# Top 32 from pairs of scores in twelve steps, a shorter first load, and more score slots in an attention and two-expert-layer kernel

## The chip, the cores and the metric

The kernel runs on one core of one Trainium2 chip. The metric is the device time of one execution in microseconds; the kernel before took a median of 808.22 us in 3 runs (807.57 to 808.52).

## The reference

Three stages run one after the other. Cut to what matters:

```python
# q, k, v: batch 2, heads 8, seq 576, head_dim 64; top_k = 32
scores = scale * q @ k.T
kth = 32nd largest of each row of scores
scores = where(scores >= kth, scores, -1e9)
attn = softmax(scores)                       # over the kept ones
x = (attn @ v), heads side by side           # 1152 tokens x 512
x = sum over 4 experts e of p[:, e] * (relu(x @ w1[e]) @ w2[e])   # F = 1024
out = ((x @ w_a) * (x @ w_b)) @ w_out        # d_ff = 1536
```

Every row of 576 scores needs its largest score and its 32nd largest one; the rest follows from these two.

## The kernel before

The 1152 tokens are cut into nine tiles of 128, and the tiles into groups of 1, 2, 3 and 3 (`GROUPS`, L28). Attention runs in 36 steps: for each group, for each of the 4 pairs of heads, for each tile of the group. So steps 0 to 3 belong to the first group, 4 to 11 to the second, 12 to 23 to the third and 24 to 35 to the fourth. A group's expert layer can be finished only when all four pairs of heads of the group are through.

One step treats one tile and two heads (x = 0, 1). TensorE makes 128x576 scores for each head (`scores`, L760, asked for `AHEAD` = 2.4 steps early); ScalarE copies them from PSUM into a score slot (L781; four slots, L513). VectorE then finds the 32 largest in `masked` (`top`, L796): four times MAX8, which gives the eight largest of a row, and between them three times MATCH_REPLACE8, which overwrites those eight by a very low number in a copy in the buffer `e` (L815). So a head takes seven passes over 576 elements. `e` has three buffers (L516). GpSimd makes two small products from the largest and the 32nd largest (L829, L833); ScalarE passes over the 576 scores three times (L839 masks, L844 takes exponentials and their sum, L855 divides by the sum); GpSimd writes one column of `e` (L874) to mark it ready, TensorE transposes it in `weigh` (L885 to L898) and multiplies it with v. The result of a pair of heads goes into `xf` (first group) or as high and low part into `xs` (L935, L937).

The operands of a step are loaded `OPERANDS` = 3 steps early: k is read in two DMAs (one for each head; the very first in four, L655), turned by TensorE, and kept in a scratch in DRAM for later groups; the last 64 rows of k of both batches lie in `krem`, filled by four DMAs with the first k (L661 to L667), for which the first transposes wait. q comes in two DMAs for a tile. All DMAs are issued by SyncE's queue (`load`, L568).

The first group's expert layer (`plain`, L1169) uses plain fp32 weights; the others (`experts`, L1007) use weights split into a high part, cast by ScalarE (L958), and a low part, subtracted by GpSimd or, where `late` is set, by VectorE (L959, L961 to L963). `late` (L1018) is set for the whole fourth group and for the last two experts of the third.

The order of the work on every engine is fixed before the program is built: each operation is entered with an engine, an expected duration, a key, what it waits for and the buffers that it uses; a planner (`Plan.order`, L216) starts on each engine the ready operation of the smallest key for which its buffers are free, and `Plan.best` (L147) keeps the best of 42 such orders. Buffers of one kind are handed out in one fixed sequence. So any change of costs, keys or slots can change the order of everything that comes after.

The seven passes, as the program enters them:

```python
for r in range(rounds):                                   # L798
    ... nc.vector.max(m8v()[:, x, cs], at())              # L809
    if r < rounds - 1:
        ... nc.vector.match_replace(out=src[1](), in_to_replace=m8v()[:, x, cs],
                                    in_values=at(), imm_value=LOW)   # L815
```

Of the kernel before, what the change touches and what calls it, by code (L numbers as in the profile page):

```python
# [16 lines left out]
DRAM = bass.MemoryType.DRAM  # L17

TOPK = 32
LOW = -3.0e38  # L20
STEEP = 2.0**80
MIX = "mix"
# [4 lines left out]
SIZES = [1, 2, 3, 3]  # L27
GROUPS = [TILES[sum(SIZES[:i]):sum(SIZES[:i + 1])] for i in range(len(SIZES))]  # L28

AHEAD = 2.4  # L30
OPERANDS = 3.0

# [376 lines left out]
TURN_F = 109  # L409
AV, SWITCH = 1092, 350  # L410
SCORE, TILED = 1944, 190
LATE = 2

FILL = 9
SLACK, EASE = 1200, 600

URGENT = 3

SOONER = (99,)

# [8 lines left out]
def body(tc, q, k, v, probs, w1, w2, wa, wb, wo, out):  # L429
# [66 lines left out]
    wscr = dr.tile([F2 // 256, 128, 2048], F32, name="wscr")  # L496

    big = Region("big", 10752, F32)
    kts = big.slots("kt", 4, WK)
    kraws = big.slots("kraw", 2, M4 * 2 * D)  # L500
    krems = big.slots("krem", 2, H * D)
    qraws = big.slots("qraw", 2, 4 * 2 * D)
    qas = big.slots("qa", 2, 4 * 128)
    mid = Region("mid", 4 * 2048 + 5 * 768, F32)
    wides = mid.slots("wide", WIDE, 2048)
    mid.again(F32R)
# [9 lines left out]
    turns = [Typed(sb, f"e{i}", 2 * S) for i in range(3)]  # L516
    es = Slots("e", turns, "e", [(i * 2 * S, (i + 1) * 2 * S) for i in range(3)])
    es.rank = 0
    m8s = low.slots("m8", 2, 2 * TOPK)
    endss = low.slots("ends", 2, 4)  # L520
    sumss = low.slots("sums", 2, 2)
    hfs = low.slots("hf", 2, 512)
# [45 lines left out]
    def load(dst, src, key, after=(), tiles=(), nbytes=1 << 18, since=0.0):  # L568


        op = plan.add("SP", 0, lambda: nc.sync.dma_start(out=dst(), in_=src()), key, after, tiles, nbytes=nbytes)  # L571
        op.since = since
        return op

    def scalar(n, emit, key, after, tiles, sbuf=False, ptr=False, extra=0):
        return plan.add("ACT", act(n, sbuf, ptr) + extra, emit, key, after, tiles, lag=110)
# [26 lines left out]
    def main_rows(x, b, h):  # L603

        return x[b, h:h + 2, 0:MAIN].rearrange("h (p m) d -> p h m d", m=M4)
# [37 lines left out]

    vrem_done, qrem_done, kept = {}, [], {}
    krem = [krems.tile() for _ in range(B)]
    krem_done = []

    def keys(b, h2, key):

        h = 2 * h2  # L650
        rt, kt = kraws.tile(key), kts.tile(key)
        rv = lambda: rt.ap.rearrange("p (m h d) -> p m h d", h=2, m=M4)
        first_ = not krem_done
        lds = []
        for m0, m1 in ((0, 2), (2, M4)) if first_ else ((0, M4),):  # L655
            for i in range(2):
                lds.append(load(
                    lambda i=i, m0=m0, m1=m1: rv()[:, m0:m1, i], lambda i=i, m0=m0, m1=m1: main_rows(k, b, h)[:, i, m0:m1],
                    key - 2, (), [rt], 32768 * (m1 - m0),
                ))  # L660
        if first_:  # L661
            for c in range(B):
                for x in range(B):
                    rs = slice((x + c) % B * REM, ((x + c) % B + 1) * REM)
                    krem_done.append(load(
                        lambda c=c, rs=rs: krem[c].ap[rs].rearrange("p (h d) -> p h d", d=D), lambda x=x: last_rows(k, x), key - 1.98, (), [krem[c]], 131072,
                    ))  # L667
        at = atts.tile(key + 0.02)

        def turn():  # L670
            a = at.ap.rearrange("p c n -> p (c n)")
            kr = [krem[c].ap[:, h * D:(h + 2) * D] for c in (1 - b, b)]
            tr(a[:, 0:128], kr[0], ident)
            for m in range(M4):
                tr(a[:, (1 + m) * 128:(2 + m) * 128], rt.ap[:, m * 128:(m + 1) * 128], ident)
            tr(a[:, 640:768], kr[1], ident)

        o = tensor(6 * TURN_F, turn, key + 0.02, lds + krem_done + [ready], [at, rt] + krem)
        av = lambda c0, c1: at.ap.rearrange("p c n -> p (c n)")[:, REM + c0:REM + c1]
        if first_:  # L680
            got = [
                scalar(HALF + REM, lambda: nc.scalar.activation(kt.ap[:, 0:HALF + REM], av(0, HALF + REM), AF.Copy), -902, [o], [at, kt]),
                vector(dve(HALF), lambda: nc.vector.tensor_copy(kt.ap[:, HALF + REM:WK], av(HALF + REM, WK)), -902, [o], [at, kt]),
            ]
        else:
            got = [scalar(WK, lambda: nc.scalar.activation(kt.ap, av(0, WK), AF.Copy), -902, [o], [at, kt])]  # L686
        if any(c for c, g in enumerate(GROUPS) if (b, h2) not in kept and c >= 0):
            kept[b, h2] = load(lambda: kscr[b, h2], lambda: kt.ap, key + 1, got, [kt], 320 << 10, since=13e3)
        return kt, got
# [7 lines left out]
    def queries(pair, n, key):  # L697

        h, T = pair.h, pair.T
        norm = [t for t in pair.tiles if t != MIX]  # L700
        rq, qa = qraws.tile(key), qas.tile(n)
        rqv = lambda: rq.ap[:, 0:len(norm) * 128].rearrange("p (m h d) -> p m h d", m=len(norm), h=2)
        lds = []
        for b in sorted({t[0] for t in norm}):
            at = [i for i, t in enumerate(norm) if t[0] == b]
            r0, w = norm[at[0]][1], len(at)
            for i in range(2):
                lds.append(load(
                    lambda a0=at[0], w=w, i=i: rqv()[:, a0:a0 + w, i], lambda b=b, r0=r0, w=w, i=i: main_rows(q, b, h)[:, i, r0:r0 + w],
                    key - 1.95, (), [rq], 32768 * w,  # L710
                ))
        if MIX in pair.tiles:
            if not qrem_done:
                for b in range(B):
                    qrem_done.append(load(lambda b=b: qrem[b * REM:(b + 1) * REM], lambda b=b: last_rows(q, b), key - 2, (), (), 131072, since=60e3))
            lds += qrem_done
        at = ms.tile() if n == 0 else atts.tile(key + 0.04)
        a = lambda: (at.ap if n == 0 else at.ap[:, 0])[:, 0:T * 128]

        def turn():  # L720
            for i, t in enumerate(pair.tiles):
                tr(a()[:, i * 128:(i + 1) * 128], qrem[:, h:h + 2].rearrange("p h d -> p (h d)") if t == MIX else rq.ap[:, i * 128:(i + 1) * 128], ident)

        o = tensor(T * TURN_F, turn, key + (0.015 if n == 0 else 0.04), lds + [ready], [at, rq])
        if n == 0:
            pair.qd = [vector(dve(128), lambda: nc.vector.tensor_copy(qa.ap[:, 0:128], a()), -903, [o], [at, qa])]
        else:
            pair.qd = [scalar(T * 128, lambda: nc.scalar.activation(qa.ap[:, 0:T * 128], a(), AF.Copy), -901, [o], [at, qa])]
        pair.q = qa

    def start_pair(c, h2, n):
# [25 lines left out]
                ]  # L757
        return pair

    def scores(pair, i, n):  # L760

        t = pair.tiles[i]
        ats, ss_ = [atts.tile(n - AHEAD + 0.001 * j) for j in range(2)], [ss.tile(n + 0.001 * j) for j in range(2)]
        parts = [(slice(0, 128), t[0])] if t != MIX else [(slice(b * REM, (b + 1) * REM), b) for b in range(B)]

        def emit():
# [20 lines left out]
    def masked(sd, n):  # L787
# [5 lines left out]
        ev = lambda x: ep.ap[:, x * S:(x + 1) * S]  # L793
        last = []

        def top(x, src, c0, rounds, width, key, done):  # L796

            for r in range(rounds):  # L798
                cs = slice(c0 + r * 8, c0 + r * 8 + 8)
                at = src[min(r, 1)]  # L800
                if n + r == 0:
# [10 lines left out]
                if r < rounds - 1:  # L812
                    done = vector(
                        132 + 1.04 * width,
                        lambda at=at, cs=cs: nc.vector.match_replace(  # L815
                            out=src[1](), in_to_replace=m8v()[:, x, cs], in_values=at(), imm_value=LOW
                        ),
                        key + 0.02 * r + 0.01, done, [m8, sd[x][0], ep],
                    )
            return done[0]  # L820

        for x in range(2):
            s = sd[x][0]
            key = n + 0.001 * x
            last.append(top(x, [lambda s=s: s.ap, lambda x=x: ev(x)], 0, TOPK // 8, S, key, sd[x][1]))
        ks = -3000 + n if n in SOONER else n + 0.1 if n > URGENT else n - 0.7
        out_, ex = [], []
        en = gpsimd(
            150, lambda: nc.gpsimd.tensor_tensor(endv(), m8v()[:, :, ::TOPK - 1], facs.unsqueeze(2).to_broadcast([128, 2, 2]), op=ALU.mult),  # L829
            -500, last + [ready], [m8, ends]  # L830
        )
        off = gpsimd(
# [174 lines left out]
    def experts(c):  # L1007
# [7 lines left out]
        yd, sums_ = {}, {}  # L1015
        for e in range(E):

            late = 2 if c == len(GROUPS) - 1 else c == len(GROUPS) - 2 and e >= LATE  # L1018
            for f0 in range(0, F, 512):
                hts, units = [], []  # L1020
                for u in range(f0, f0 + 512, 256):
# [448 lines left out]
```

## Time and profile before

| | |
|---|---|
| median of 3 runs | 808.22 us (807.57 to 808.52) |
| the profiled execution | 808.02 us, of which the profile's span is 806.2 us |
| TensorE busy | 771.0 us (96%), mean granted clock 0.998 |
| VectorE busy | 731.9 us (91%) |
| ScalarE busy | 508.0 us (63%) |
| GpSimd busy | 238.0 us (30%) |
| chain that ended last | TensorE 87%, VectorE 7%, DMA 2% |

Busy time is that of the engine's own instructions; instructions of the sequencers (waits, DMA issues) are not in it. The chain is followed back from the last instruction, at each step to what released it. The span is divided in the page into 40 slices of some 20 us; TensorE's busy tenths in them begin 5, 6, 8 and are 9 in all later ones but the eighth and the last, which are 8.

### The profile page before, as it was taken

Reading aid. Unit: us, or ns where it says so; the run is one execution under the profiler, and the core shown is the slowest. Engines: PE = TensorE matmul, PEld = TensorE weight load, DVE = VectorE, ACT = ScalarE, POOL = GpSimd, SP = SyncE. Lnnn points to the kernel's source line nnn. Section 1 sums busy time; section 2 is a strip of 40 time slices with the busy share of each in tenths; the row PEclk is TensorE's granted clock in tenths of the full one; section 3 lists DMA queues with packets and bytes.
Section 4 is the critical chain, followed back from the end, with each engine's and each line's share of the span. In section 5 each row is a group of like instructions: output and inputs, shape, how many; then the busy total and the mean of one; then the engine's idle time right before and its main releaser. Section 6 shows DMA issues by size and latency. Waiting matters only on the chain.

```text
span 806.2 us, 14094 instructions
## 1 busy us (share of the span) xinstructions
PE 771.0 (96%) x5145; PEld 673.1 (83%) x5145; DVE 731.9 (91%) x1425; ACT 508.0 (63%) x871; POOL 238.0 (30%) x289
## 2 busy tenths in 40 slices
PE   5689999899999899999999999999999999999998
PEld 3477776688888778888899998899988989899996
DVE  4999999999999999999998599898899899999755
ACT  2688778899898889776675657566545533233110
POOL 0000014475666526430000001321224334343121
PEclk9999999999999999999999999999999999999999
DMA  5875887445654343433324455889521413313013
GB/s 146 264 260 162 291 254 237 151 141 182 199 164 159 107 143 105 142 127 102 109 78 131 157 172 170 271 296 323 180 106 42 137 32 106 124 34 105 0 54 117
DMA packets 100037, 122.57 MB, mean 152 GB/s; under 512 B 26624, under 2 KB 73728, under 8 KB 98432
## 3 DMA queue, kind: packets, MB, share of 16 engines
q1 hardware_dynamic: 99968, 121.67, 46.9%
q8 instruction: 40, 0.66, 0.4%
q14 instruction: 29, 0.24, 0.1%
HBM read 110.38 MB, written 11.27 MB: 151 GB/s over the span
## 4 chain that ended last, share of the span: by engine, by line
PE 87%; DVE 7%; DMA 2%; ACT 1%; SPq 1%; issue 0%; POOL 0%; DVEq 0%; ACTq 0%
PE ps L589 83%; PE ps L592 4%; DVE low L809 3%; DVE e L815 2%; DMA mid<-in_moe_w_dram 2%; SPq L571 1%; ACT lowa L901 0%; DMA big<-in_k_dram 0%; DVE mid_again L1031 0%; DVE xs L1163 0%; DVE low L1056 0%; ACT big L686 0%; ACT e L855 0%; ACT lowa L781 0%; DVE e L1272 0%
## 5 line engine op out<-in xcount | busy, mean ns | idle before, releaser
L589 PE MATMUL ps<-mid_again 128*128 128x512 f32 x1092 | 262.9, 393 | 0.0
L589 PEld LDWEIGHTS ps<-mid_again 128*128 128x128 f32 x1092 | 201.2, 188 | 43.8 <-issue 4.7
L589 PE MATMUL ps<-xs,mid_again 128*128 128x384 f32 (+1 forms) x1152 | 192.3, 320 | 4.7 <-DVE xs L1163 2.1
L589 PEld LDWEIGHTS ps<-xs,mid_again 128*128 128x128 f32 x1152 | 181.5, 189 | 12.4 <-issue 4.5
L809 DVE MAX8 low<-e 128x8 f32<-128x576 f32 x216 | 154.5, 748 | 0.0
L959 POOL TENSOR_TENSOR mid_again<-raw,mid_again 128x1024 fp32r<-128x1024 f32 x48 | 114.8, 2402 | 25.5 <-ACT mid_again L958 23.2
L958 ACT ACTIVATE mid_again<-raw 128x1024 fp32r<-128x1024 f32 x96 | 101.1, 1057 | 19.7 <-PE ps L589 12.6
L815 DVE MATCH_REPLACE8 e<-low,e 128x576 f32<-128x576 f32 x144 | 106.1, 743 | 0.0
L1275 POOL TENSOR_TENSOR low<-e,e 128x512 int32<-128x512 int32 x36 | 50.0, 1389 | 161.1 <-DVE e L1272 113.3
L589 PE MATMUL ps<-xs,big_again 128*128 128x320 f32 (+1 forms) x576 | 86.4, 297 | 0.2 <-DVE low L1364 0.2
L589 PEld LDWEIGHTS ps<-xs,big_again 128*128 128x128 f32 x576 | 80.3, 190 | 1.1 <-DVE low L1364 0.4
L589 PE MATMUL ps<-lowa_again,big_again 128*128 128x320 f32 (+1 forms) x432 | 66.4, 296 | 1.4 <-ACT rest L1373 1.1
L959 DVE TENSOR_TENSOR mid_again<-raw,mid_again 128x1024 fp32r<-128x1024 f32 x48 | 62.2, 1301 | 5.0 <-ACT mid_again L958 4.8
L1027 ACT ACTIVATE mid_again<-ps 128x384 fp32r<-128x384 f32 (+1 forms) x96 | 43.3, 455 | 33.6 <-PE ps L589 32.9
L589 PEld LDWEIGHTS ps<-lowa_again,big_again 128*128 128x128 f32 x432 | 60.8, 190 | 2.5 <-ACT rest L1373 1.3
L839 ACT ACTIVATE e<-lowa,low 128x576 f32<-128x576 f32 x72 | 53.1, 776 | 13.7 <-POOL low L829 13.3
L855 ACT ACTIVATE e<-e,low 128x576 f32<-128x576 f32 x72 | 52.7, 772 | 11.1 <-DVE low L852 11.0
L844 ACT ACTIVATE e<-e,low 128x576 f32<-128x576 f32 x72 | 55.6, 775 | 0.8 <-POOL low L833 0.7
L1031 DVE SCALAR_TENSOR_TENSOR mid_again<-ps,mid_again 128x384 fp32r<-128x384 f32 (+1 forms) x96 | 48.3, 506 | 7.4 <-ACT mid_again L1027 6.7
L1364 DVE TENSOR_TENSOR low<-ps,low 128x256 f32<-128x256 f32 (+1 forms) x105 | 43.7, 447 | 11.4 <-PE ps L589 10.8
L815 DVE MATCH_REPLACE8 e<-low,lowa 128x576 f32<-128x576 f32 x72 | 53.1, 743 | 0.0
L781 ACT ACTIVATE lowa<-ps 128x576 f32<-128x576 f32 x72 | 42.9, 644 | 13.0 <-PE ps L589 9.0
(110 smaller groups left out, 1013.2 us busy)
## 6 DMA issues: line engine op xcount, KB each, us to landing
raw<-in_moe_w_dram SPq DMA_DIRECT2D x116, 512.0 KB, 4.0
big<-kscr SPq DMA_DIRECT2D x20, 320.0 KB, 4.0
low<-in_v_dram SPq DMA_DIRECT2D x24, 256.0 KB, 3.7
e<-in_moe_w_b_dram SPq DMA_DIRECT2D x12, 512.0 KB, 4.2
e<-in_moe_w_a_dram SPq DMA_DIRECT2D x12, 512.0 KB, 3.9
e<-in_moe_w_out_dram SPq DMA_DIRECT2D x12, 512.0 KB, 4.3
wscr<-big_again SPq DMA_DIRECT2D x6, 1024.0 KB, 5.6
mid_again<-wscr SPq DMA_DIRECT2D x6, 1024.0 KB, 4.9
```

The source lines that it names most:

```text
L589: nc.tensor.matmul(out, l, r, **kw)
L809: 62 + 1.04 * width, lambda at=at, cs=cs: nc.vector.max(m8v()[:, x, cs], at()), key + 0.02 * r, [done],
L815: lambda at=at, cs=cs: nc.vector.match_replace(out=src[1](), in_to_replace=m8v()[:, x, cs], in_values=at(), imm_value=LOW),
L839: S, lambda x=x, s=s: nc.scalar.activation(ev(x), s.ap, AF.Prelu, bias=endv()[:, x, 1:2], scale=scale, alpha=STEEP),
L844: lambda x=x: nc.scalar.activation(ev(x), ev(x), AF.Exp, bias=endv()[:, x, 0:1], accum_out=sums.ap[:, x:x + 1]),
L855: S, lambda x=x: nc.scalar.activation(ev(x), ev(x), AF.Copy, scale=sums.ap[:, x:x + 1]),
L958: hi = scalar(1024, lambda: nc.scalar.activation(u.ap[:, 0:1024], r.ap, AF.Copy), 500 + s, [ld], [u, r], sbuf=True)
L959: sub = lambda eng: eng.tensor_tensor(u.ap[:, 1024:2048], r.ap, u.ap[:, 0:1024], op=ALU.subtract)
L1027: n, lambda h=h, p=p: nc.scalar.activation(h.ap[:, 0:n], p.ap[:, 0:n], AF.Relu), -1000, [o], [h, p]
L1031: lambda h=h, p=p: nc.vector.scalar_tensor_tensor(h.ap[:, n:2 * n], p.ap[:, 0:n], 0.0, h.ap[:, 0:n], op0=ALU.max, op1=ALU.subtract),
L1275: return gpsimd(pool_(512), lambda: nc.gpsimd.tensor_tensor(t().bitcast(I32), fold(c.ap.bitcast(I32)), fold(lowv().bitcast(I32)), op=ALU.a ...
L1364: return vector(dve(m), lambda: nc.vector.tensor_tensor(tv(out), p.ap[:, 0:m], tv(i), op=ALU.add), K, [o] + after, [p, tp])
```

## The change

- **First loads.** The first k is one DMA of both heads. The first `krem` part is only what the first pair of heads needs: of the 64 rows of the step's own batch one DMA for each copy, one issued by SyncE and one by ScalarE, the other 64 rows being set to zero by GpSimd; the remaining six DMAs for `krem` follow. The first q is one DMA, issued by ScalarE. Later k and one-tile q are one DMA instead of two.
- **Pairs of scores.** In steps 0 to 11 (without head 0 of step 0) the row is folded: VectorE takes the larger of score i and score i + 288 (`larger`), GpSimd adds the bit patterns of the two as integers (`added`) and subtracts the larger one (`smaller`), each over 288 elements. The top 32 of the larger ones take four MAX8 and three MATCH_REPLACE8 over 288, the top 16 of the smaller ones two and one. At most 16 of the 32 largest scores can be smaller ones of their pair, so the 32nd largest is the minimum over sixteen maxima of one sorted list against the other reversed: two small VectorE operations for a step. The three folding operations are asked for 1.99 steps early and use the step's buffer `e`. The first MATCH_REPLACE8 of the larger ones waits for `smaller` (`guard`).
- **Slots and keys.** Ten score slots instead of four, five k buffers instead of four; scores asked for 4.4 steps early, operands 5.
- **Low parts.** `late` is now set for the last two experts of the fourth group alone.

The diff, cut to its core:

```diff
+WM = 3 * TOPK // 2 + 2
-AHEAD = 2.4
-OPERANDS = 3.0
+AHEAD = 4.4
+OPERANDS = 5.0
-LATE = 2
+FOLD = range(12)
-    kts = big.slots("kt", 4, WK)
+    kts = big.slots("kt", 5, WK)
+    ss2 = big.slots("s2", 6, S)
-    m8s = low.slots("m8", 2, 2 * TOPK)
+    m8s = low.slots("m8", 2, 2 * WM)
+    def load_by_act(dst, src, key, tiles=()):
+        return plan.add("ACT", 100, lambda: nc.scalar.dma_start(out=dst(), in_=src()), key, (), tiles, lag=LAND)
...
-        for m0, m1 in ((0, 2), (2, M4)) if first_ else ((0, M4),):
-            for i in range(2):
-                lds.append(load(
-                    lambda i=i, m0=m0, m1=m1: rv()[:, m0:m1, i], lambda i=i, m0=m0, m1=m1: main_rows(k, b, h)[:, i, m0:m1],
-                    key - 2, (), [rt], 32768 * (m1 - m0),
-                ))
+        lds = [load(rv, lambda: pair_rows(k, b, h), key - 2, (), [rt])]
...
+                gpsimd(200, lambda c=c, blank_=blank_: nc.gpsimd.memset(krem[c].ap[blank_, 0:2 * D], 0.0), -1e5, [], [krem[c]])
+            krem_done[0] = [plan.ops[-1], plan.ops[-2], last(1, 0, 0, 2, key - 1.98), last(0, 0, 0, 2, -1e5, True)]
+            rest_ = [last(c, x, 2, H, key - 1.9) for x in range(B) for c in range(B)]
+            krem_done[1] = [last(c, 1, 0, 2, key - 1.9) for c in range(B)] + rest_
...
+            if n == 0:
+                lds.append(load_by_act(lambda: rqv()[:, 0], lambda b=b, r0=r0: pair_rows(q, b, h)[:, r0], -1e6, [rq]))
+            elif w == 1:
+                lds.append(load(lambda a0=at[0]: rqv()[:, a0], lambda b=b, r0=r0: pair_rows(q, b, h)[:, r0], key - 1.95, (), [rq], 65536))
...
+        folds = [x for x in range(2) if n in FOLD and (n, x) != (0, 0)]
         for x in range(2):
...
+            kf = n - 1.99 + 0.001 * x
+            added = gpsimd(pool_(HALF), lambda halves=halves, low_=low_: whole(nc.gpsimd, ALU.add, low_(), *halves()), kf, [sd[x][1]], [s, ep])
+            larger = vector(
+                dve(HALF) + 30, lambda halves=halves, high=high: nc.vector.tensor_tensor(high(), *halves(), op=ALU.max), kf, [sd[x][1]], [s, ep], port=True
+            )
+            smaller = gpsimd(
+                pool_(HALF), lambda high=high, low_=low_: whole(nc.gpsimd, ALU.subtract, low_(), low_(), high()), kf, [added, larger], [ep]
+            )
+            t = top(x, [high], [8 * r for r in range(TOPK // 8)], key, larger, smaller)
+            last.append(top(x, [low_], [TOPK, TOPK + 8], key + 0.09, smaller))
+            last[-1].waits.append(t)
+        if folds:
+            xs_ = slice(folds[0], folds[-1] + 1)
+            a = vector(
+                100, lambda: nc.vector.tensor_tensor(
+                    m8v()[:, xs_, TOPK // 2:TOPK], m8v()[:, xs_, TOPK // 2:TOPK], m8v()[:, xs_, 3 * TOPK // 2 - 1:TOPK - 1:-1], op=ALU.max
+                ), n + 0.15, last[folds[0]:], [m8]
+            )
+            last.append(vector(
+                100, lambda: nc.vector.tensor_reduce(
+                    out=m8v()[:, xs_, WM - 2:WM - 1], in_=m8v()[:, xs_, TOPK // 2:TOPK], axis=mybir.AxisListType.X, op=ALU.min
+                ), n + 0.16, [a], [m8]
+            ))
...
-            late = 2 if c == len(GROUPS) - 1 else c == len(GROUPS) - 2 and e >= LATE
+            late = 2 if c == len(GROUPS) - 1 and e >= 2 else 0
```

## Rows read from the trace of the kernel before

**Rows 1.** Windows: stretch, length, busy PE, PEld, DVE, ACT, POOL; clock; DMA share.
```profile
0.00:13.00 13.00, 6.13 (x24) 4.62 (x24) 1.29 (x4) 1.75 (x2) 1.94 (x11) 1.00 0.51 114
13.00:60.00 47.00, 33.49 (x232) 25.90 (x230) 46.48 (x100) 32.17 (x62) 2.65 (x15) 1.00 0.81 254
60.00:133.00 73.00, 72.14 (x527) 52.43 (x528) 71.63 (x159) 56.93 (x107) 11.64 (x32) 1.00 0.77 234
133.00:166.00 33.00, 28.63 (x201) 22.80 (x199) 32.74 (x72) 29.58 (x53) 14.74 (x19) 0.95 0.56 178
...
255.00:295.00 40.00, 36.02 (x273) 30.40 (x274) 39.52 (x86) 33.95 (x60) 16.54 (x20) 1.00 0.45 145
295.00:460.00 165.00, 165.00 (x1175) 144.89 (x1174) 151.84 (x289) 120.98 (x204) 36.82 (x56) 1.00 0.36 114
```

**Rows 2.** Chain that ended last: start us, length us, what.
```profile
4.88 3.44 DMA big<-in_k_dram
...
163.00 1.46 DVE e L815 x2
...
276.77 1.46 DVE e L815 x2
```

**Rows 3.** Timeline of DVE, 150 to 153 and 290 to 291: start, length.
```profile
150.89 0.41 DVE L937 TENSOR_TENSOR xs<-ps,xs 128x256 fp32r<-128x256 f32 x1
...
290.43 0.54 DVE L937 TENSOR_TENSOR xs<-ps,xs 128x384 fp32r<-128x384 f32 x1
```

**Rows 4.** Timeline of all engines, first 14 us.
```profile
0.71 4.80 SPq L571 DMA_DIRECT2D big<-in_k_dram  x8
...
5.56 1.09 SPq L571 DMA_DIRECT2D big<-in_q_dram  x2
...
8.45 1.73 PE L592 MATMUL ps<-identr,big 128*128 128x128 f32 x7 [4.16 <-DMA big<-in_k_dram]
...
10.88 2.29 PE L589 MATMUL ps<-big 64*128 64x288 f32 x8 [0.70 <-DVE big L726]
...
13.17 1.43 DVE L804 MAX8 low<-ps 128x8 f32<-128x576 f32 x2 [2.44 <-PE ps L589]
```

**Rows 5.** Timeline of DVE, 85 to 89 us: issue times of neighbours.
```profile
85.83 0.74 DVE L809 MAX8 low<-e 128x8 f32<-128x576 f32 x1
86.49 0.07 DVE L815 MATCH_VALUE_LOAD e<-low,e 128x8 f32 x1
...
87.21 0.08 DVE L815 MATCH_VALUE_LOAD e<-low,e 128x8 f32 x1
...
87.93 0.41 DVE L937 TENSOR_TENSOR xs<-ps,xs 128x256 fp32r<-128x256 f32 x1
88.26 0.15 DVE L852 RECIPROCAL low<-low 128x2 f32<-128x2 f32 x1
88.34 1.40 DVE L809 MAX8 low<-e 128x8 f32<-128x576 f32 x2
```

**Rows 6.** Single lines on POOL: durations in ns, least/median/most.
```profile
L1275 POOL TENSOR_TENSOR low<-e,e x36: 1300/1314/2087, 460.8 to 741.3; 128x512 int32<-128x512 int32 x36
L1367 POOL TENSOR_TENSOR low<-low x30: 735/876/1797, 613.2 to 790.8; 128x256 f32<-128x256 f32 x18, 128x320 f32<-128x320 f32 x12
```

**Rows 7.** Groups on DVE, 60 to 100 us, then 200 to 250: busy, mean ns.
```profile
L809 DVE MAX8 low<-e 128x8 f32<-128x576 f32 x24 | 16.9, 746 | 0.0
...
L809 DVE MAX8 low<-e 128x8 f32<-128x576 f32 x25 | 17.9, 749 | 0.0
```

**Rows 8.** Timeline of POOL, 132 to 135 us: step 11's products.
```profile
133.59 0.20 POOL L829 TENSOR_TENSOR low<-low,facs 128x4 f32<-128x4 f32 x1
```

**Rows 9.** Timeline of PE, 139 to 172 us: step 11's transposes.
```profile
144.67 1.09 PE L592 MATMUL ps<-identr,e 128*128 128x128 f32 x9
```

**Rows 10.** Line L959 on POOL and on DVE: durations in ns.
```profile
L959 POOL TENSOR_TENSOR mid_again<-raw,mid_again x48: 2354/2407/2445, 128.4 to 353.9; 128x1024 fp32r<-128x1024 f32 x48
L959 DVE TENSOR_TENSOR mid_again<-raw,mid_again x48: 1204/1218/2307, 363.4 to 575.5; 128x1024 fp32r<-128x1024 f32 x48
```

More of the change, by code (lines that the diff above doesn't have):

```diff
@@ L645, in body @@
     krem = [krems.tile() for _ in range(B)]
-    krem_done = []
+    krem_done = {}
     def keys(b, h2, key):
@@ L653, in keys, with last @@
         first_ = not krem_done
-        lds = []
-        for m0, m1 in ((0, 2), (2, M4)) if first_ else ((0, M4),):
-            for i in range(2):
-                lds.append(load(
-                    lambda i=i, m0=m0, m1=m1: rv()[:, m0:m1, i], lambda i=i, m0=m0, m1=m1: main_rows(k, b, h)[:, i, m0:m1],
-                    key - 2, (), [rt], 32768 * (m1 - m0),
-                ))
+        lds = [load(rv, lambda: pair_rows(k, b, h), key - 2, (), [rt])]
+        def last(c, x, h0, h1, key, act=False):
+            rs = slice((x + c) % B * REM, ((x + c) % B + 1) * REM)
+            dst, src = lambda: krem[c].ap[rs, h0 * D:h1 * D].rearrange("p (h d) -> p h d", d=D), lambda: last_rows(k, x)[:, h0:h1]
+            return load_by_act(dst, src, key, [krem[c]]) if act else load(dst, src, key, (), [krem[c]], 16384 * (h1 - h0))
         if first_:
             for c in range(B):
[L663 to L667, printed above, removed]
+                blank_ = slice((1 - c) * REM, (2 - c) * REM)
+                gpsimd(200, lambda c=c, blank_=blank_: nc.gpsimd.memset(krem[c].ap[blank_, 0:2 * D], 0.0), -1e5, [], [krem[c]])
+            krem_done[0] = [plan.ops[-1], plan.ops[-2], last(1, 0, 0, 2, key - 1.98), last(0, 0, 0, 2, -1e5, True)]
+            rest_ = [last(c, x, 2, H, key - 1.9) for x in range(B) for c in range(B)]
+            krem_done[1] = [last(c, 1, 0, 2, key - 1.9) for c in range(B)] + rest_
+            krem_done[1][0].waits += krem_done[0][:2]
+            krem_done[1][1].waits += krem_done[0][:2]
+        done = krem_done[0] if first_ else krem_done[0] + krem_done[1]
         at = atts.tile(key + 0.02)
@@ L676, in turn @@
             tr(a[:, 640:768], kr[1], ident)
-        o = tensor(6 * TURN_F, turn, key + 0.02, lds + krem_done + [ready], [at, rt] + krem)
+        o = tensor(6 * TURN_F, turn, key + 0.02, lds + done + [ready], [at, rt] + krem)
         av = lambda c0, c1: at.ap.rearrange("p c n -> p (c n)")[:, REM + c0:REM + c1]
@@ L706, in queries @@
             r0, w = norm[at[0]][1], len(at)
[L707 to L711, printed above, removed]
+            if n == 0:
+                lds.append(load_by_act(lambda: rqv()[:, 0], lambda b=b, r0=r0: pair_rows(q, b, h)[:, r0], -1e6, [rq]))
+            elif w == 1:
+                lds.append(load(lambda a0=at[0]: rqv()[:, a0], lambda b=b, r0=r0: pair_rows(q, b, h)[:, r0], key - 1.95, (), [rq], 65536))
+            else:
+                for i in range(2):
+                    lds.append(load(
+                        lambda a0=at[0], w=w, i=i: rqv()[:, a0:a0 + w, i], lambda b=b, r0=r0, w=w, i=i: main_rows(q, b, h)[:, i, r0:r0 + w],
+                        key - 1.95, (), [rq], 32768 * w,
+                    ))
         if MIX in pair.tiles:
@@ L758, in start_pair, with scores_slot @@
         return pair
+    scored = []
+    def scores_slot(need):
+        scored.append(0)
+        return (ss if len(scored) % 10 < 4 else ss2).tile(need)
     def scores(pair, i, n):
         t = pair.tiles[i]
-        ats, ss_ = [atts.tile(n - AHEAD + 0.001 * j) for j in range(2)], [ss.tile(n + 0.001 * j) for j in range(2)]
+        ats, ss_ = [atts.tile(n - AHEAD + 0.001 * j) for j in range(2)], [scores_slot(n + 0.001 * j) for j in range(2)]
         parts = [(slice(0, 128), t[0])] if t != MIX else [(slice(b * REM, (b + 1) * REM), b) for b in range(B)]
@@ L794, in masked, with top @@
         last = []
[L796 to L801, printed above, removed]
+        def top(x, src, cols, key, done, guard=None):
+            for r, c0 in enumerate(cols):
+                cs = slice(c0, c0 + 8)
+                at = src[min(r, len(src) - 1)]
+                width = S if len(src) == 2 else HALF
+                if n + r == 0 and len(src) == 2:
                     bank, scored = sd[x][2:]
@@ L811, in top @@
                     )]
-                if r < rounds - 1:
+                if r < len(cols) - 1:
+                    to = src[min(1, len(src) - 1)]
                     done = vector(
                         132 + 1.04 * width,
-                        lambda at=at, cs=cs: nc.vector.match_replace(
-                            out=src[1](), in_to_replace=m8v()[:, x, cs], in_values=at(), imm_value=LOW
+                        lambda at=at, cs=cs, to=to: nc.vector.match_replace(
+                            out=to(), in_to_replace=m8v()[:, x, cs], in_values=at(), imm_value=LOW
                         ),
-                        key + 0.02 * r + 0.01, done, [m8, sd[x][0], ep],
+                        key + 0.02 * r + 0.01, done + ([guard] if r == 0 else []), [m8, sd[x][0], ep],
                     )
             return done[0]
+        folds = [x for x in range(2) if n in FOLD and (n, x) != (0, 0)]
         for x in range(2):
@@ L824, in masked @@
             key = n + 0.001 * x
-            last.append(top(x, [lambda s=s: s.ap, lambda x=x: ev(x)], 0, TOPK // 8, S, key, sd[x][1]))
+            if x not in folds:
+                cols = [8 * r for r in range(TOPK // 8 - 1)] + [WM - 9]
+                last.append(top(x, [lambda s=s: s.ap, lambda x=x: ev(x)], cols, key, sd[x][1]))
+                continue
+            halves = lambda s=s: (s.ap[:, 0:HALF], s.ap[:, HALF:S])
+            high, low_ = (lambda x=x, i=i: ev(x)[:, i * HALF:(i + 1) * HALF] for i in range(2))
+            whole = lambda e, op, out, a, b: e.tensor_tensor(out.bitcast(I32), a.bitcast(I32), b.bitcast(I32), op=op)
+            kf = n - 1.99 + 0.001 * x
[20 more added lines that the diff above has]
+                ), n + 0.16, [a], [m8]
+            ))
         ks = -3000 + n if n in SOONER else n + 0.1 if n > URGENT else n - 0.7
@@ L828, in masked @@
         en = gpsimd(
-            150, lambda: nc.gpsimd.tensor_tensor(endv(), m8v()[:, :, ::TOPK - 1], facs.unsqueeze(2).to_broadcast([128, 2, 2]), op=ALU.mult),
+            150, lambda: nc.gpsimd.tensor_tensor(endv(), m8v()[:, :, 0:WM - 1:WM - 2], facs.unsqueeze(2).to_broadcast([128, 2, 2]), op=ALU.mult),
             -500, last + [ready], [m8, ends]
```

## The prediction

> **What bounds the kernel now.** I read the stretches first, then the chain, then the two places where the chain leaves TensorE. From 295 to 460 us TensorE is busy for all of 165.00 us, so there it is the bound and nothing on another engine counts [rows 1]. Ahead of 295 us it is not: it sits idle for 13.00 - 6.13 = 6.9 us up to 13 us, 47.00 - 33.49 = 13.5 us up to 60, 0.9 us up to 133, 4.4 us up to 166 and 4.0 us from 255 to 295, together 29.7 us. In every one of those stretches but the first VectorE is full: 46.48 of 47.00, 71.63 of 73.00, 32.74 of 33.00, 39.52 of 40.00. The chain says the same: at 163 us and again at 277 us it runs through MATCH_REPLACE8 on VectorE [rows 2]. So TensorE gets its work at a pace that the top 32 sets, until two joins: the last high and low split of the second group at 150.89 us and of the third at 290.43 us [rows 3]. After the second join TensorE has enough to do to the end. The time saved is therefore how much sooner VectorE brings the second join, as long as TensorE has done by then what lies ahead of it.
>
> **First loads.** SyncE issues eight DMAs in 4.80 us, the eighth at 4.88 us, and it is 3.44 us until that has landed [rows 2]; the first transposes start at 8.45 us, the first scores at 10.88 us, the first MAX8 at 13.17 us [rows 4]. After the change SyncE issues two ahead of the transposes, the second at about 0.71 + 0.60 = 1.31 us; with the same 3.44 us that is 4.75 us, 3.6 us sooner. That is the best case. ScalarE issues the other two; its queue has nothing else to do before the transposes but its table load (1.75 us busy in the first 13 us [rows 1]). If both issues stand behind that, the second goes out at 0.71 + 1.3 + 0.6 = 2.6 us and lands at 6.1 us; allowing 0.5 us for a bigger DMA it is 6.6 us, and the gain 1.7 us. I take 3.0, nearer to the best, since the eight old DMAs carried more bytes than the four new ones. The two q DMAs on SyncE (1.09 us) leave its queue, and the six rest ones of krem take their place ahead of step 1, so step 1 is loaded about when it was; step 0 covers it with some 9 us of VectorE work.
>
> **The fold.** VectorE's price is the distance from one start to the next: MAX8 over 576 takes 86.49 - 85.83 = 0.66 us, a MATCH_REPLACE8 with its value load 0.72 us, a two-input operation over 256 elements 0.33 us, a reciprocal of two columns 0.08 us [rows 5]. A head costs 4 x 0.66 + 3 x 0.72 = 4.80 us now. From 576 and 256 elements follows 0.33 us for 320 elements, so 288 elements fewer save 0.30 us: a MAX8 over 288 is put at 0.36, a MATCH_REPLACE8 at 0.42, the maximum at 0.36 us. These are estimates from those rows. A folded head has six MAX8, four MATCH_REPLACE8 and one maximum: 2.16 + 1.68 + 0.36 = 4.20 us. That is 0.60 us less, for 23 heads 13.8 us. Halving the width saves so little because the number of passes rises from seven to eleven.
>
> **What it adds.** Two small operations a step, 24 in all: 0.08 us each by the reciprocal (1.9 us), 0.33 by the 256-wide operation (7.9 us); at 32 elements they lie near the first, so 0.10 each, 2.4 us. GpSimd gets 46 operations over 288 elements: the 256-wide ones on it took from 0.735 us, the integer ones over 512 took 1.31 [rows 6], which gives about 0.81 us each, 37 us in all, in 120 us in which it is now busy for some 16 us. MAX8 does not feel GpSimd: 746 ns where GpSimd is nearly idle, 749 ns from 200 to 250 us, where it is at work most of the time [rows 7]. The two-input maximum may: GpSimd's two-input operations, beside two-input work on VectorE, reached 2.09 us against 1.30 at least [rows 6]. I take 0.08 us for each of the 23 maxima, 1.8 us. The bounds are 0 and a whole GpSimd operation, 0.81 us, so 0 to 18.6 us. The Trainium skill's page "SBUF — State Buffer", section "Who interferes with whom", speaks against the change here: a VectorE instruction with two SBUF inputs and a GpSimd instruction that reads SBUF lock each other out for the whole of an instruction. By that rule at its worst the upper bound holds each time, and the sum would have 18.6 us in place of 1.8. The longest durations are of the kind that it asks for, the medians are not.
>
> **Buffers and queues.** The fold needs buffer `e` early. Step 11's products start at 133.59 us and its transposes at 144.67 us, so a buffer is held for some 12 us after its top 32 is found [rows 8, 9]. Between the end of step n and the start of step n + 3 VectorE has two steps; twelve take 133.59 - 13.17 = 120.4 us now [rows 4, 8], 10.0 each, and some 8.9 after the fold, so about 17.7 us. The 5.7 us left hold the four GpSimd operations of a step (3.2 us). So the fold is covered, by 2 to 3 us; if the cover goes, VectorE waits at the guard. ScalarE is at 56.93 of 73 us, 78% [rows 1]; with shorter steps it goes to about 88%, and stays cover. Six more score slots and earlier keys add no work; scores made earlier fill some of TensorE's idle 13.5 us before 60 us (up to 2 us, taken as nothing). Wider k loads cost nothing on SyncE, there are fewer of them.
>
> **Low parts.** 32 subtractions go from VectorE (1.22 us) to GpSimd (2.41 us) [rows 10]: 39 us off one, 77 us on the other, all after 350 us. There TensorE is full and GpSimd was busy for 36.82 of 165 us, so I put this at nothing; it may give back up to 2 us of small waits, or lose 1 if low parts come late.
>
> **The sum.** VectorE at the joins: -3.0 - 13.8 + 2.4 + 1.8 = -12.6 us. Steps 12 to 23 are as before, so the second join moves by the same. TensorE can follow: the start gives it 3.0 us, steps 0 to 3 another 7 x 0.60 - 0.9 = 3 us of its idle time, and the idle 4.4 and 4.0 us at the joins are there for the rest, 14.4 us in all. The clock, at 0.95 of full from 133 to 166 us [rows 1], would give back up to 1.7 us with the idle time there. 808.0 us for the profiled execution less 12.6 is 795.4; half a microsecond for a rough first step makes it 796. The profiled execution stands 0.2 us under the median of the runs, which I leave out.
>
> **Rivals.** *The fold waits (0.14).* If the 2 to 3 us of cover are not there, the first MATCH_REPLACE8 of the larger ones waits for GpSimd's addition and subtraction, 1.62 us, under which only the maximum and one MAX8, 0.72 us, can go: 0.9 us for each head in which nothing else is ready. When it comes to half of them the fold's net 9.6 us are gone and only the first loads stay: 804.5. For it: three `e` buffers; against it: the other head's passes. *TensorE is not waiting for the join (0.10).* Only the early idle time is won, about 6 us: 802. For it, 60 to 133 us, where TensorE is already full. *More (0.12).* Scores ahead and the relief of VectorE after 350 us come on top: 791 down to 788. *Slower by the lock (0.08).* If each maximum waits for a whole GpSimd operation, which the page named above would have at its worst, VectorE loses 18.6 us in place of 1.8: 795.4 + 16.8 = 812. It decides from 0.08 + 12.6 / 23 = 0.63 us a maximum on. Against it: a planner that does not start the two together, and the medians of rows 6.
>
> **Numbers.** 0.56 stays for the forecast (791 to 801). The range 788 to 805 takes in the forecast, TensorE's case, most of the waiting fold and the edge of "more". A measurement here tells no less than 0.2%, 1.6 us, from no change. Faster 0.86, the same 0.05 (the waiting fold at its worst), slower 0.09.
>
> **What would show it.** Right: the first MAX8 near 10 us, MAX8 over 288 at intervals of 0.36 us, step 11's products near 121 us, the second join near 278 us, VectorE without gaps until then. Wrong: gaps on VectorE ahead of a MATCH_REPLACE8 with GpSimd as releaser, maxima of over 1 us, or TensorE's idle time at the joins as large as now.

## The result, and the profile after

The changed kernel took a median of 798.06 us in 4 runs (797.39 to 798.52); beside it the kernel before took 808.37. The ratio is 0.9864, with a 95% interval of 0.9846 to 0.9882: about 10 us faster. The profiled execution took 797.67 us, its span is 795.9 us, 10.3 less than before.

The windows of the changed kernel, in the stretches of [rows 1] (length; busy PE, PEld, DVE, ACT, POOL; clock; DMA share, GB/s):

```profile
0.00:13.00 13.00, 6.31 (x24) 4.65 (x24) 2.00 (x5) 1.75 (x2) 2.35 (x13) 1.00 0.58 136
13.00:60.00 47.00, 35.58 (x227) 26.03 (x228) 46.25 (x156) 32.89 (x64) 20.60 (x37) 0.67 0.80 251
60.00:133.00 73.00, 72.53 (x555) 54.26 (x555) 72.34 (x260) 62.12 (x117) 27.51 (x57) 1.00 0.76 235
133.00:166.00 33.00, 33.00 (x229) 25.82 (x227) 32.39 (x71) 31.59 (x57) 20.72 (x20) 1.00 0.67 216
166.00:255.00 89.00, 88.98 (x711) 77.00 (x714) 87.86 (x193) 80.41 (x144) 57.42 (x54) 1.00 0.54 164
255.00:295.00 40.00, 39.26 (x299) 33.36 (x292) 39.52 (x85) 35.01 (x63) 21.29 (x21) 1.00 0.50 155
295.00:460.00 165.00, 165.00 (x1169) 147.26 (x1168) 137.79 (x275) 120.28 (x202) 87.12 (x76) 1.00 0.39 123
```

Over the whole span TensorE's busy time hardly changed (771.0 us before, 770.2 now), while its idle time went from 35.2 to 25.7 us: nearly all of the gain is waiting that is gone. From 13 to 60 us it is idle for 2.1 us less, and at the joins for 4.4 less from 133 to 166 and 3.2 less from 255 to 295. In the page of the kernel before, the fourteenth slice (262 to 282 us, ahead of the second join) is an 8 as well as the eighth and the last; the eighth and the fourteenth are 9 now. The two joins on VectorE, in its timeline, come 8.5 and 8.7 us sooner than in [rows 3]:

```profile
142.39 0.42 DVE L993 TENSOR_TENSOR xs<-ps,xs 128x256 fp32r<-128x256 f32 x1
...
281.75 0.55 DVE L993 TENSOR_TENSOR xs<-ps,xs 128x384 fp32r<-128x384 f32 x1
```

The start, from the timeline of all engines, to be read against [rows 4]. SyncE now issues nine DMAs for k and `krem` in a row, and the transposes begin at 7.92 us, only 0.53 us sooner; the first MAX8 comes at 12.38 for 13.17:

```profile
0.72 6.23 SPq L574 DMA_DIRECT2D big<-in_k_dram  x9
0.72 0.43 ACTq L580 DMA_DIRECT2D big<-in_q_dram  x1
...
7.92 1.51 PE L599 MATMUL ps<-identr,big 128*128 128x128 f32 x6 [3.84 <-DMA big<-in_k_dram]
...
10.06 2.29 PE L596 MATMUL ps<-big 64*128 64x288 f32 x8 [0.19 <-DVE big L694]
...
12.38 0.77 DVE L827 MAX8 low<-ps 128x8 f32<-128x576 f32 x1 [2.38 <-PE ps L596]
```

Step 11's products, at 133.59 us in [rows 8], come 7.0 us sooner in GpSimd's timeline. VectorE is further ahead than that: it has by then done some 1.4 us more of step 12's passes than before, which makes up nearly all of the 8.5 us at the first join.

```profile
126.56 0.19 POOL L885 TENSOR_TENSOR low<-low,facs 128x4 f32<-128x4 f32 x1 [0.45 <-DVE low L878]
```

### The profile page after: what moved, and what is told of

It reads as the page before. It is cut to its first block, busy times and chain, and to the rows that moved or that the text cites. A ratio compares the mean times of both kernels' runs of the same rounds, so it can differ in the third digit from the quotient of the medians.

```text
span 795.9 us, 14267 instructions
## 1 busy us (share of the span) xinstructions
PE 770.2 (97%) x5145; PEld 673.3 (85%) x5145; DVE 695.8 (87%) x1532; ACT 506.6 (64%) x871; POOL 354.8 (45%) x369
## 4 chain that ended last, share of the span: by engine, by line
PE 90%; DVE 8%; SPq 1%; ACT 0%; issue 0%; DMA 0%; POOL 0%
PE ps L596 86%; PE ps L599 4%; DVE low L832 3%; DVE e L839 2%; DVE e L862 1%; SPq L574 1%; DMA big<-in_k_dram 0%; DVE low L1112 0%; DVE low L873 0%; DVE xs L1177 0%; ACT lowa L957 0%; ACT e L895 0%; DVE low L827 0%; DVE low L1420 0%; DVE raw L1465 0%
## 5 line engine op out<-in xcount | busy, mean ns | idle before, releaser
L1015 POOL TENSOR_TENSOR mid_again<-raw,mid_again 128x1024 fp32r<-128x1024 f32 x80 | 192.6, 2414 | 77.7 <-ACT mid_again L1014 75.9
L832 DVE MAX8 low<-e 128x8 f32<-128x576 f32 (+1 forms) x285 | 160.9, 599 | 0.0
L839 DVE MATCH_REPLACE8 e<-low,e 128x576 f32<-128x576 f32 (+1 forms) x190 | 112.1, 595 | 0.0
L911 ACT ACTIVATE e<-e,low 128x576 f32<-128x576 f32 x72 | 53.1, 773 | 10.4 <-DVE low L908 10.3
L596 PE MATMUL ps<-big 64*128 64x288 f32 (+1 forms) x320 | 51.7, 470 | 3.8 <-ACT big L744 3.1
L1423 POOL TENSOR_TENSOR low<-low 128x256 f32<-128x256 f32 (+1 forms) x30 | 28.9, 963 | 50.2 <-DVE low L1420 49.1
L957 ACT ACTIVATE lowa<-ps 128x512 f32<-128x512 f32 x72 | 42.8, 645 | 6.7 <-PE ps L599 6.6
L1373 ACT ACTIVATE big_again<-low 128x768 fp32r<-128x768 f32 (+1 forms) x24 | 22.8, 949 | 32.1 <-POOL low L1331 29.4
```

The lines of the kernel that those rows point to most:

```text
L596: nc.tensor.matmul(out, l, r, **kw)
L839: lambda at=at, cs=cs, to=to: nc.vector.match_replace(out=to(), in_to_replace=m8v()[:, x, cs], in_values=at(), imm_value=LOW),
L911: S, lambda x=x: nc.scalar.activation(ev(x), ev(x), AF.Copy, scale=sums.ap[:, x:x + 1]),
L957: w, lambda j=j, w=w, at=at: nc.scalar.activation(p.ap[:, j * MAIN:j * MAIN + w], at.ap.rearrange("p b n -> p (b n)")[:, j * (MAIN - 128): ...
L1015: sub = lambda eng: eng.tensor_tensor(u.ap[:, 1024:2048], r.ap, u.ap[:, 0:1024], op=ALU.subtract)
```

## The experiments

"Join" is the start of the third group's last split on VectorE (line L993, or its neighbour), "rest" the span from there to the end, both from the profiled execution. "Ratio" is against the kernel before, run beside it. A profiled execution is one of several: its time is 806.27 us in run 1, where the median is 808.56, and 797.11 in run 10, where it is 794.36.

| kernel | ratio (95% interval) | first MAX8 | join | rest |
|---|---|---|---|---|
| before | | 13.17 | 290.4 | 515.8 |
| changed | 0.9864 (0.9846 to 0.9882) | 12.38 | 281.8 | 514.1 |
| 1 no fold | 0.9989 (0.9973 to 1.0006) | 11.80 | 290.0 | 514.2 |
| 2 old slots and keys | 0.9926 (0.9901 to 0.9951) | 12.29 | 284.7 | 516.5 |
| 3 old first loads | 0.9869 (0.9839 to 0.9899) | 13.11 | 283.1 | 513.4 |
| 4 `krem` loads behind | 0.9825 (0.9796 to 0.9853) | 9.22 | 279.3 | 514.1 |
| 5 GpSimd does not read | 0.9847 (0.9828 to 0.9867) | 11.87 | 280.3 | 513.5 |
| 6 24 folded steps | 1.0003 (0.9992 to 1.0013) | 12.49 | 293.5 | 513.9 |
| 7 old low parts | 0.9849 (0.9831 to 0.9866) | 12.36 | 281.9 | 513.6 |
| 8 other random numbers | 0.9857 (0.9840 to 0.9874) | 12.52 | 282.3 | 513.4 |
| 9 as 6, GpSimd's fold light | 0.9991 (0.9974 to 1.0008) | 12.32 | 294.1 | 513.9 |
| 10 as 4, planned anew | 0.9820 (0.9786 to 0.9854) | 9.16 | 280.7 | 514.6 |
| 11 as 6, low parts do not read | 0.9899 (0.9883 to 0.9916) | 12.04 | 284.3 | 513.9 |

The last column is the main finding. In thirteen kernels the end lies 513.4 to 514.6 us behind the join, but for the two with the old slots, where it is 515.8 and 516.5. Those two have started 224 score matmuls before the join, the others 238 or 240: the scores of some two steps, which TensorE then has still to make. Behind the join it is busy for 509.7 and 510.0 us in those two and for 507.3 to 508.3 in the others.

**1. No fold.**

```diff
-FOLD = range(12)
+FOLD = range(0)
```

> The changed kernel with no folded step; first loads, slots, keys and low parts as changed. Theory A (VectorE's pace sets both joins, and the fold is what quickens it): VectorE needs 4.9 us a head again instead of 4.4, step 11's products come at 132 to 134 us instead of 126.6, the second join near 289 us, TensorE is idle for some 8 us around the joins again, time 804 to 807. Theory B (the gain is scores made ahead in TensorE's idle first 60 us, by more slots and earlier keys): most of the gain stays, 798 to 801.

Measured: 808.56 us, no different from before. Step 11's products come at 133.5 us, the join at 290.0. Theory A held for the joins; the median is a little over its range. Without the fold the other parts together are worth nothing that can be measured, so theory B fell.

**2. Old slots and keys.**

```diff
-AHEAD = 4.4
-OPERANDS = 5.0
+AHEAD = 2.4
+OPERANDS = 3.0
-    kts = big.slots("kt", 5, WK)
+    kts = big.slots("kt", 4, WK)
-        return (ss if len(scored) % 10 < 4 else ss2).tile(need)
+        return ss.tile(need)
```

> The changed kernel with four score slots, four k buffers and the keys of before (scores 2.4 steps ahead, operands 3). Theory A: the fold still quickens VectorE; TensorE loses the two steps of scores that it made ahead before 60 us (2.3 us), of which the joins hide a part: 799 to 801. Theory B: nearly all is lost, 805 to 808. If the fold cannot start early enough, VectorE shows gaps ahead of the first MATCH_REPLACE8 of a folded head, with GpSimd as releaser, and it is 803 or more.

Measured: 803.04 us, between the two theories, and with the gaps that the last sentence of the expectation names. 3.0 us of the loss lie at the join: VectorE was busy for 44.12 of the 47 us from 13 to 60, 46.25 in the changed kernel. 2.4 us are the rest. VectorE's timeline shows two of the waits:

```profile
41.25 1.43 DVE L862 TENSOR_TENSOR e<-lowa 128x288 f32<-128x288 f32 x2 [0.90 <-ACT lowa L803]
...
44.13 0.09 DVE L839 MATCH_VALUE_LOAD e<-low,e 128x8 f32 x1 [0.72 <-POOL e L858]
```

The maxima wait for the copy of their scores, and the first MATCH_REPLACE8 behind them waits at the guard for GpSimd's subtraction: the rival of the waiting fold, in small. The other parts without the fold give nothing (run 1); with the fold the slots and keys are worth some 5 us. Which of them does it, score slots, k buffers or keys, is not separated.

**3. Old first loads.** The functions for the first k, `krem` and q as before, all else as changed.

> The changed kernel with the first loads (and the two DMAs for k and for q) of before. The first MAX8 of the changed kernel came only 0.8 us sooner than before (12.38 for 13.17 us). Theory A: this part of the change is worth that and no more: first MAX8 near 13.2 us, time 798 to 800. Rival (it was worth the 3 us of the prediction, by some other way): 801 or more.

Measured: 798.16 us. This part of the change, as it stands, brought nothing that can be measured.

**4. The two loads over zeroed rows behind the first transposes.** Every engine keeps its order but SyncE.

```diff
+    behind = krem_done[1][:2]
     for op in plan.best():
+        if op in behind:
+            continue
         op.emit()
+        if op is turned_[0]:            # the first transposes
+            for b in behind:
+                b.emit()
```

> The changed kernel, every engine's order kept, but the two loads of krem that write over the rows set to zero are issued behind the first transposes. Theory: in the changed kernel the first transposes waited for the last of the eight first DMAs on SyncE (7.83 us landed, 7.92 started), because these two are issued ahead and write rows that the transposes read. Moved behind, the transposes wait for k and the two small loads alone (landed by 4.8 us): they start at 4.9 to 5.3 us, the first MAX8 at 9.5 to 10 us. If VectorE's start is what counts, the time falls by 2 to 3 us, to 795 to 796.5; if TensorE has no idle time left at the joins to give (0.7 us from 255 to 295 us), it stays at 797 to 798.5. Rival for the start: the transposes still start near 7.9 us, as the DMAs are only slow.

Measured: 795.11 us. From its timeline of all engines:

```profile
4.76 1.51 PE L599 MATMUL ps<-identr,big 128*128 128x128 f32 x6 [0.68 <-DMA big<-in_k_dram]
...
6.90 2.29 PE L596 MATMUL ps<-big 64*128 64x288 f32 x8 [0.20 <-DVE big L695]
...
9.22 0.77 DVE L828 MAX8 low<-ps 128x8 f32<-128x576 f32 x1 [2.38 <-PE ps L596]
```

The transposes start 3.2 us sooner, and the span is 2.5 us shorter. The intervals of the two ratios overlap a little, but the longest execution of this kernel (795.24 us) is shorter than the shortest of the changed one (797.39). So the change had zeroed half of the rows in order not to wait for them, and then issued the loads into these very rows ahead of the transposes, which therefore waited for the last of eight DMAs after all. The early start was there to be had.

**5. GpSimd's part of the fold without reading.**

```diff
-  ... whole(nc.gpsimd, ALU.add, low_(), *halves())
+  ... nc.gpsimd.memset(low_(), 0.0)
-  ... whole(nc.gpsimd, ALU.subtract, low_(), low_(), high())
+  ... whole(nc.gpsimd, ALU.subtract, low_()[:, 0:8], low_()[:, 0:8], low_()[:, 8:16])
```

> The changed kernel, every engine's order kept; GpSimd's addition over 288 becomes a memset of the same 288 elements (which reads nothing) and its subtraction one over 8 elements. It leaves out the smaller ones of the pairs: their list is taken from zeros. In the changed kernel 9 of the 23 maxima on VectorE took 0.5 to 1.0 us to the next start, the others 0.37; all 23 together 12.2 us where 23 x 0.365 is 8.4. Theory (a maximum waits while GpSimd reads from SBUF): all 23 now take 0.37, VectorE gains 3.8 us before step 11's products, and the time falls by 3 to 4 us, to 794 to 795. Rival (the long maxima have another cause, such as their scores being late): nothing changes there, 797 to 798.5.

Measured: 796.81 us. The 23 maxima, in ns (least/median/most), first in the changed kernel, then in this one, from the view of their line:

```profile
L862 DVE TENSOR_TENSOR e<-big x13: 436/450/1046, 20.5 to 113.4; 128x288 f32<-128x288 f32 x13
L862 DVE TENSOR_TENSOR e<-lowa x10: 436/444/918, 15.4 to 112.7; 128x288 f32<-128x288 f32 x10
```

```profile
L862 DVE TENSOR_TENSOR e<-big x13: 456/460/491, 19.5 to 111.4; 128x288 f32<-128x288 f32 x13
L862 DVE TENSOR_TENSOR e<-lowa x10: 440/454/485, 14.9 to 111.1; 128x288 f32<-128x288 f32 x10
```

From each start to the next they cost 12.2 us in all, and 9.4 here. These sums hold some idle time of VectorE behind a maximum, 0.55 and 0.79 us, nearly all of it spent waiting for ScalarE; without it they are 11.6 and 8.6 us. So eight maxima waited in the changed kernel, not nine, for 3.2 us in all, and 3.0 of these are gone here. Each of the eight ends 0.31 or 0.32 us behind the end of a GpSimd addition or subtraction that was running when it started, as this one does (VectorE, then GpSimd, in the changed kernel):

```profile
48.36 0.89 DVE L862 TENSOR_TENSOR e<-big 128x288 f32<-128x288 f32 x1
```

```profile
48.13 0.80 POOL L858 TENSOR_TENSOR e<-lowa 128x288 int32<-128x288 int32 x1
```

Step 11's products come at 124.6 us, 2.0 sooner, half a microsecond of it from a sooner first MAX8. They do not gain more because VectorE, quicker now, stands idle for 3.6 us between its first MAX8 and these products, in place of 1.4. The join moves by 1.5 us and the median by 1.3, less than expected, and the intervals of the two ratios overlap; what is shown is the waiting, not its price in the end.

**6. Twenty-four folded steps.** `FOLD = range(24)`, planned anew.

> The changed kernel with 24 folded steps instead of 12. Between 60 and 460 us TensorE was idle for 1.2 us altogether in the changed kernel. Theory A as it stands now: with TensorE full from 60 us on, a quicker VectorE after step 11 has nothing left to give: 797 to 799. Rival (VectorE's pace still counts at the second join): 12 more steps at 0.5 us a head less, up to 10 us: 788 to 794.

Measured: 809.11 us. Both theories missed: it is not that nothing is gained, all is lost. The join is 11.8 us later. From 166 to 255 us GpSimd is almost full (80.36 us busy, 57.42 with twelve folded steps) and TensorE short of work (84.62, 88.98 with twelve):

```profile
166.00:255.00 89.00, 84.62 (x636) 72.66 (x637) 82.47 (x247) 73.88 (x130) 80.36 (x77) 0.98 0.52 163
```

**9. The same with GpSimd's part light** (the edit of run 5 on run 6). The first suspicion was GpSimd's additions.

> The kernel with 24 folded steps, every engine's order kept, but GpSimd's addition a memset and its subtraction over 8 elements, as in the run without the lock; it leaves out the smaller ones of the pairs. With 24 folded steps GpSimd was busy for 80.4 of 89 us from 166 to 255 us (57.4 with twelve), step 14 to 23 took some 12 us each, and the second join came at 293.5 us. Theory: GpSimd's additions and subtractions (0.8 us each) stand in one queue with the low parts (2.4 us each), and folded steps wait for both; without them the steps fall under 10.5 us and the second join comes at 276 to 283 us, time 790 to 799. Rival (the order that the planner found for 24 steps is poor by itself, or ScalarE limits): the second join stays at 288 or later, time 803 or more.

Measured: 808.67 us, join at 294.1: this theory fell. The timeline of run 6, VectorE and then GpSimd, showed another cause:

```profile
175.98 2.29 DVE L873 TENSOR_TENSOR low<-low 128x32 f32<-128x32 f32 x1
```

```profile
175.81 2.40 POOL L1015 TENSOR_TENSOR mid_again<-raw,mid_again 128x1024 fp32r<-128x1024 f32 x1
```

The small maximum over 32 elements starts 0.17 us behind a low part on GpSimd and ends at 178.27 us, GpSimd's at 178.21.

**11. The low parts without reading.**

```diff
-            lo = gpsimd(pool_(1024), lambda: sub(nc.gpsimd), -100, [hi], [u, r])
+            def blank_low():
+                nc.gpsimd.memset(u.ap[:, 1024:2048].bitcast(F32), 0.0)
+                nc.gpsimd.memset(u.ap[:, 1024:2048].bitcast(F32), 0.0)
+            lo = gpsimd(pool_(1024), blank_low, -100, [hi], [u, r])
```

> The kernel with 24 folded steps, every engine's order kept, additions and subtractions as they are, but each low part of the experts' weights on GpSimd (2.4 us, two reads from SBUF) becomes two memsets of the same 1024 elements, which read nothing; it leaves out those low parts. The theory that GpSimd's additions are what folded steps 12 to 23 pay fell with the last run: without them the second join stayed at 294.1 us. New theory: the two-input operations of VectorE wait behind low parts. With 24 folds the small maximum at a step's end (a last link before the products) took 0.86 us on average instead of 0.09 in steps 12 to 23, 8.5 us too much in 12, up to 2.3 us each, and the large maxima 4.7 us too much in 22; the twelve unfolded steps have no such operation. Without reads in the low parts the small maximum takes 0.1 us, the second join comes at 276 to 285 us, time 790 to 799. Rival (the order for 24 folds is poor by itself): second join at 289 or later, time 804 or more.

Measured: 800.91 us, join at 284.3. The small maximum's line in runs 6, 9 and 11:

```profile
L873 DVE TENSOR_TENSOR low<-low x24: 163/193/2289, 24.6 to 273.5; 128x32 f32<-128x32 f32 x23, 128x16 f32<-128x16 f32 x1
```

```profile
L873 DVE TENSOR_TENSOR low<-low x24: 158/177/2404, 23.8 to 272.2; 128x32 f32<-128x32 f32 x23, 128x16 f32<-128x16 f32 x1
```

```profile
L873 DVE TENSOR_TENSOR low<-low x24: 151/176/601, 23.6 to 264.0; 128x32 f32<-128x32 f32 x23, 128x16 f32<-128x16 f32 x1
```

9.2 of the 11.8 us come back at the join, 8.2 in the time, which lands 1.9 us past the upper end of the expectation. Two memsets take 1.91 us where a low part takes 2.42, so GpSimd is also freer, 70.4 us busy of 89 in place of 80.4. That is not what brought the join back: in run 9 GpSimd was freer still, 64.4 us, with the low parts as they were, and the join stayed at 294.1. The last 2.5 us at the join stay open.

**7 and 8. Old low parts; other random numbers.** Run 7 sets `late` as before, run 8 draws `random.Random(r + 1000)` in the planner.

> The changed kernel with the low parts on VectorE where they were before (32 subtractions from GpSimd back to VectorE). Prediction: worth nothing, since all of it lies after the second join, where TensorE is full: 797 to 800. Rival: VectorE falls behind again after 300 us and TensorE's small waits come back: 800.5 or more.

> The changed kernel with other random numbers in the planner's 42 orders, nothing else. It measures what a new order by itself is worth, as every edit that changes costs, keys or slots gets one. Theory: under 2 us either way, 796 to 800; if it is 4 us or more, the differences of the re-planned experiments cannot be read as those of their parts.

Measured: 797.00 and 797.59 us, both ratios inside each other's interval and that of the changed kernel. Moving the low parts was worth nothing that can be measured. A new set of orders by itself, in the one that was tried, moved the time by half a microsecond, so differences of several microseconds between re-planned runs can be read as those of their parts.

**10. The loads behind, planned anew.** The two loads get the first transposes as something they wait for.

> The changed kernel in which the two loads of krem over the zeroed rows wait for the first transposes in the plan itself, so that every order is made anew from it. Theory: the same head start as with the orders kept (first MAX8 near 9.2 us), the second join near 279 us, and end = second join + 514 us as in all runs so far: 794 to 796 with what lies around the span. Rival: the new order loses the head start on the way, 797 or more.

Measured: 794.36 us. It is level with run 4 (795.11), and these two have the lowest medians; against the kernel before, 1.8% less, where the change has 1.4%.

## Why the prediction was right, point by point

The prediction said 796.0 us, 788 to 805; the median is 798.06. What bounds the kernel was read rightly: the time is the join and some 514 us behind it. That the number came so close is in part luck, as two errors of opposite sign stand in it. By the sum's terms:

- **First loads, -3.0 us:** the step that failed. It named the DMAs that the transposes need and took SyncE's first two as all of them, but the planner put the loads into the zeroed rows ahead of the transposes too. The start came 0.8 us sooner. The bounds were 1.7 and 3.6, so the measured value lay outside them. Run 4 shows 3.2 us of head start with the cause removed. That kernel's transposes start at 4.76 us where the best case was 4.75, which is in part chance: SyncE's second DMA was issued later than estimated (1.54 us, not 1.31) and landed after 3.1 us, not 3.44.
- **The passes, -13.8 us:** right, within a microsecond. In the group view of VectorE up to step 11 the changed kernel has

```profile
L832 DVE MAX8 low<-e 128x8 f32<-128x288 f32 x138 | 55.6, 443 | 0.0
L839 DVE MATCH_REPLACE8 e<-low,e 128x288 f32<-128x288 f32 x92 | 39.9, 439 | 0.0
```

  and from start to start a MAX8 over 288 costs 0.364 us, a MATCH_REPLACE8 with its value load 0.42, close to the 0.36 and 0.42 estimated from 576 and 256 elements. With 0.365 for the maximum a folded head costs 4.25 us; by the same count a head cost 4.82 before. That is 0.57 us less for each of the 23, 13.2 in all.
- **Small operations, +2.4 us:** 2.9 measured, 0.7 of it one operation that waited for GpSimd.
- **Contention, +1.8 us:** the term that was mis-sized; 3.2 us. It had been drawn from a mean stretch, 0.08 us for every maximum. In truth 15 of the 23 paid nothing and 8 waited for the rest of a GpSimd operation, up to 0.6 us. The page "SBUF — State Buffer" of the Trainium skill, section "Who interferes with whom", has the rule that the prediction weighed: the ports that the two engines share are an exclusive lock, for which a VectorE instruction with two SBUF inputs contends with a GpSimd instruction that reads SBUF. The runs agree with it, most plainly in run 6, where 32 elements took 2.29 us behind GpSimd's 2.40. What kept the price low in the changed kernel is that two thirds of the maxima did not wait and the others only for the rest of an operation of some 0.8 us, not that a meeting is cheap. The rival that rested on this rule, 812 us, did not come true with twelve steps; with 24 its mechanism did, with GpSimd's low parts in place of its additions.
- **The sum at the second join:** -12.6 predicted, -8.7 measured. With the measured -0.8, -13.2, +2.9 and +3.2 the sum gives -7.9; the 0.8 us that are left have no term.
- **Scores ahead, taken as nothing:** another 1.7 us, the rest of 514.1 for 515.8. At the join the prediction promised 3.9 us too much, and here 1.7 too little, which is why 796 was close.
- **Buffers and the guard:** right; VectorE's one gap of over 0.6 us between 13 and 300 us is 0.71 us in step 0. From the first MAX8 to step 11's products a step takes 9.5 us on average; the 8.9 of the prediction left out its own small operations and waits, with which it is 9.2. The waiting fold came only with the old slots (run 2), so the slots that the prediction put at nothing are part of its cover.
- **Low parts, at nothing:** right (run 7).
- **TensorE not waiting for the join (802):** it fell; the idle time at the joins went down by 7.6 us, and in run 1, where the joins stayed, the time stayed too.
- **The signs that it named:** the intervals of MAX8 came as said. The first MAX8 (12.38 us for 10), step 11's products (126.56 for 121) and the second join (281.75 for 278) all came later, and one maximum, at 1.05 us, was of the kind named as a sign of being wrong.

## What to carry to other kernels

Find the moment from which the bounding engine is all but full to the end, and price every edit by how much sooner it brings that moment: here a span of 793 to 808 us was that moment plus 513 to 517. A load that is meant to be out of the way must also be issued behind the work that it should not hold up, else a write into the same rows makes that work wait. A small two-input operation on VectorE at the end of a chain lasts until the GpSimd operation that it meets, one that reads SBUF, is through (here 2.29 us for 32 elements), so a trick that pays where GpSimd is free can cost all of its gain where GpSimd has long operations to do.

## What was not expected

The granted clock of the changed kernel's profile is 0.67 from 13 to 60 us. It was at the lower level of 1.2 GHz from 16 to 44 us and at 2.4 GHz again from 48 us on; TensorE had sat idle for 3.84 us ahead of the first transposes, and it was busy for all of the stretch from 40 to 48 us, in which the clock rose. In run 8 it idled for 3.96 us there and the clock stayed at 1.00, so what made it fall is not shown. It did not cost time: of its four executions those with a mean clock of 0.98 took 797.67 and 797.39 us, those with 0.998 and 0.999 took 798.52 and 798.45. From 16 to 40 us TensorE is busy for 14.7 of 24 us and waits for VectorE, which is full.

And more of a good thing reversed: 12 folded steps gained 10 us over none, 24 gained nothing.
